# Gated recurrence and convolution gate on one core: decay constants without the logarithm table, and another written-out order

## The chip, the cores and the metric

The kernel runs on one core of a Trainium2 chip. The metric is device microseconds of one execution, lower is better. Three runs of the kernel before the change took 296.58, 295.05 and 296.55 us; their median, 296.55 us, is the time before.

The engines are called by the names of the profile: PE (TensorE; PEld is its weight load), DVE (VectorE), ACT (ScalarE), POOL (GpSimd) and SP (SyncE, which here only issues transfers). A q behind a name is that engine's queue.

## What is computed

Four sequences of 6336 tokens with 256 channels, all in float32. A recurrence with a data-dependent decay is followed by a gated linear unit:

```
a_base = sigmoid(a_param)
log_a  = 8 * sigmoid(r_gate) * log(clip(a_base, 1e-6, 1 - 1e-6))
a_t    = exp(log_a)
x_gated = sqrt(max(1 - a_t * a_t, 1e-6)) * sigmoid(i_gate) * x
h[t] = a_t[t] * h[t-1] + x_gated[t]            # y = h, zero at the start of a sequence
gate = sigmoid(sum over k < 5 of conv_w[k] * y[t - 4 + k])
out  = (gate * (y @ w_val)) @ w_out            # both 256 x 256
```

Sigmoids are computed as (1 + tanh(z/2))/2, so that the factor of the exponent is khf = 4 * log(clip(a_base)), and a_t = exp(khf * tanh(r/2) + khf).

## The kernel before

The 25,344 tokens are cut into 51 windows (two of 256 tokens at the start, one at the end, all others 512), and these into 28 chunks: chunks 0, 1, 2 and 26, 27 are one window each, and every other chunk c is the two windows 2c-3 and 2c-2. Square roots are taken in 12 batches of up to three chunks, because each needs ACT's square-root table and the way back needs the table of Exp and Tanh: two switches a batch. Batches 0 to 3 share one pair, so the loop makes 18 table loads (L518), and the setup makes two (L186, L234).

Tokens lie on the partitions when they are loaded, and channels on the partitions for the recurrence, so PE transposes three times. The work on a window or chunk is a chain of small operations, each a function op_xx of the code with a two-letter word:

- SP: lr, li, lx load r_gate, i_gate and x of a window (L278) into rings of four windows each; st stores a window (L502). s_wl.0 to s_wl.3 load the weights (L252 to L258).
- ACT: ta and tb, the tanh of the r and i gates of a chunk (L296, L299); ex, the Exp that reads the transposed tanh from PSUM (L359); rt, the square roots of a batch (L386); tg, the tanh of the convolution's result (L458); ca, a copy of a result from PSUM (L491); sa, a square (L375).
- POOL: pp, 1 + tanh of the i gate (L306); up, that times x (L318); sq, squares of a_t (L367); s_wcast, the weights to bfloat16.
- PE: tr, transposes of ta's result (L343); nt, of the square roots (L401); xt, of the gated x (L417); cv, the convolution as products with diagonals (L451); vl (L466) and ou (L481), the two matrix products; xp, x into PSUM.
- DVE: xg, the square root times the gated x (L408); sc, the recurrence as a scan of half the channels (L439); gv, gate times value (L471); cd, a copy of a result from PSUM (L489); uv, the gated x of a few early windows (L332).

The chain is lr, ta, tr, ex, sq, rt, nt, xg (with li, tb, pp, lx, up beside it), xt, sc, then cv, tg, vl, gv, ou, cd or ca, st. In a word such as ex.4.1@6,7 the first number is the chunk (of lr, li, lx, pp, up, cv, tg, vl, gv, ou, ca, cd and st: the window; of rt: the batch), the second the half of the channels, and the numbers behind the @ are PSUM banks.

The order is written out by hand: ORDER is a list of 961 words, and the loop behind it (L513) issues them one after the other. Each engine runs its own words in the order in which they stand, and waits with semaphores for what it needs; no scheduler moves anything. So the list sets five queues, the banks (which decide whose readers a matmul must wait for) and, by ca or cd, the engine of each copy. SP's queue holds loads and stores alike: a store that waits for its copy holds the loads that stand behind it, and a load waits until its slot in the ring is free, which for lr and li is when ta or tb of the window four before is done, and for lx when its product is.

The decay constants are made in s_kt: PE turns a_param onto the partitions, ACT takes an Exp, DVE three small operations, ACT a logarithm from the table set natural_log_exp_and_others (loaded at L186), then the set exp_and_others is loaded (L234) and DVE multiplies by 4.

Of the kernel before, what the change touches and what calls it, by code (L numbers as in the profile page):

```python
# [8 lines left out]
P = 128  # L9
CONV_K = 5  # L10
FP32 = mybir.dt.float32
BF16 = mybir.dt.bfloat16
ACT = mybir.ActivationFunctionType
ALU = mybir.AluOpType

CHUNKS = [[256], [256], [512], [512, 512], [512, 512], [512, 512], [512, 512], [512, 512], [512, 512], [512, 512], [512,
    512], [512, 512], [512, 512], [512, 512], [512, 512], [512, 512], [512, 512], [512, 512], [512, 512], [512,
    512], [512, 512], [512, 512], [512, 512], [512, 512], [512, 512], [512, 512], [512], [256]]
BATCHES = [[0], [1], [2], [3, 4], [5, 6, 7], [8, 9, 10], [11, 12, 13], [14, 15, 16], [17, 18, 19], [20, 21, 22], [23, 24,
    25], [26, 27]]  # L20
# [11 lines left out]
GROUPS = [[0], [1], [2], [3, 4], [5, 6], [7, 8], [9, 10], [11], [12], [13, 14], [15, 16], [17, 18], [19, 20], [21], [22],  # L32
    [23, 24], [25], [26], [27]]

ORDER = """
s_ident s_small s_kt s_diag lr.0 ta.0 lr.1 ta.1 li.0 tr.0.1@0 tb.0 pp.0 tr.0.0@1 ex.0.1 tr.1.0@2 tr.1.1@3 lr.2 ta.2
ex.1.0 tr.2.1@0 ex.1.1 ex.2.1 tr.2.0@2 lr.3 lr.4 lr.5 ex.0.0 ta.3 lr.6 ta.4 li.1 tr.3.1@0,1 lx.1 tb.1 sq.2.1 sq.1.1
sq.0.1 ex.2.0 li.2 tr.3.0@2,3 li.4 lx.0 li.3 tb.2 xp.1@4 sq.0.0 sq.1.0 sq.2.0 up.0 uv.1 lr.7 lr.8 ex.3.1 sq.4.1 ex.3.0
sq.3.0 lr.9 lr.10 lx.2 lx.4 s_wl.2 lx.3 li.5 li.6 s_wl.1 tb.3 s_wl.3 s_wl.0 ta.5 lx.5 ta.6 lr.14 rt.0 xp.2@2,3 nt.0@4
xg.0 xt.0@0,1 li.8 li.7 uv.2 rt.1 rt.2 nt.1@4 nt.2@5 xg.2 xg.1 pp.4 sq.3.1 sq.4.0 lx.6 rt.3 lr.11 tb.4 lr.12  # L40
tr.5.0@6,7 ex.5.0 xt.1@5,4 li.9 lr.13 sc.0.0 sc.0.1 pp.3 up.4 lx.8 nt.3@2,3 xt.2@0,1 sc.1.0 li.10 up.3 sc.1.1 xg.3
xt.3@2,3 tb.5 cv.1@4,5 sc.2.1 lx.7 sc.2.0 tg.1 cv.0@6,7 tg.0 tr.5.1@0,1 ex.5.1 s_wcast vl.1@4,5 sc.3.1 sc.3.0 xp.6@6,7
vl.0@0,1 nt.4@2,3 li.12 pp.5 ta.7 lr.16 sq.5.0 sq.6.0 up.5 li.11 ta.8 pp.8 uv.6 tb.6 gv.0 ou.0.0@0 lr.15 cv.2@6,7 tg.2
# [58 lines left out]
def kernel(  # L102
# [11 lines left out]
    nc = tc.nc  # L114
    B, S, D = x.shape
    H = D // P
# [63 lines left out]
    const = ctx.enter_context(tc.tile_pool(name="const", bufs=1))  # L180
# [4 lines left out]
    with tc.manual_schedule():  # L185
# [4 lines left out]
        khf = const.tile([P, H], FP32, name="khf")  # L190
# [359 lines left out]
```

## Time and profile before

| what | before |
|---|---|
| three runs, median | 296.55 us (295.05 to 296.58) |
| span of the profiled execution, first to last instruction | 294.6 us |
| the three runs above that span | 0.5 to 2.0 us |
| ACT busy | 277.3 us, 202 instructions |
| DVE, POOL, PE busy | 241.5, 241.8, 241.6 us |
| moved by DMA | 104.7 MB, mean 355 GB/s |
| mean granted PE clock | 0.990 |

The profile is one execution; a time of its own, besides the span, is not given with it. Engines run beside each other, so busy times are not added. A row of the timeline is: start in us, length in us, engine, line, operation, tile written and tile read with shapes, and in brackets the idle time of the engine just before and what ended it. A row with xN holds N instructions that followed each other. Rows on ACT overlap by about 0.1 us, so that two tanh rows of 1.91 us start 1.80 us apart. A row of the stretches gives the width in us, then busy us and instruction count of PE, PEld, DVE, ACT and POOL, the granted clock, the busy share of the DMA engines (it can pass 1 where packets overlap) and GB/s.

### The profile page before, as it was taken

Reading aid. Unit: us, or ns where it says so; the run is one execution under the profiler, and the core shown is the slowest. Engines: PE = TensorE matmul, PEld = TensorE weight load, DVE = VectorE, ACT = ScalarE, POOL = GpSimd, SP = SyncE. Lnnn points to the kernel's source line nnn. Section 1 sums busy time; section 2 is a strip of 40 time slices with the busy share of each in tenths; the row PEclk is TensorE's granted clock in tenths of the full one; section 3 lists DMA queues with packets and bytes.
Section 4 is the critical chain, followed back from the end, with each engine's and each line's share of the span. In section 5 each row is a group of like instructions: output and inputs, shape, how many; then the busy total and the mean of one; then the engine's idle time right before and its main releaser. Section 6 shows DMA issues by size and latency. Waiting matters only on the chain.

```text
span 294.6 us, 6238 instructions
## 1 busy us (share of the span) xinstructions
PE 241.6 (82%) x2497; PEld 165.2 (56%) x2497; DVE 241.5 (82%) x198; ACT 277.3 (94%) x202; POOL 241.8 (82%) x161
## 2 busy tenths in 40 slices
PE   2263879778697899988969889989889998899993
PEld 1241556436464767666636647566648674767652
DVE  2000697867999899997999998999999999999981
ACT  6799999999999999999999899999999999999754
POOL 1559979999999799999997989999997999666200
PEclk9999999999999999997999999999999999999998
DMA  7999999999999999999988999999999999965336
GB/s 242 336 414 388 383 408 401 403 412 376 414 398 405 401 383 388 392 356 417 385 257 312 364 411 414 415 350 406 374 389 384 392 331 369 346 249 209 153 142 249
DMA packets 29994, 104.74 MB, mean 355 GB/s; under 512 B 3335, under 2 KB 3854, under 8 KB 29966
## 3 DMA queue, kind: packets, MB, share of 16 engines
q1 hardware_dynamic: 29952, 104.35, 92.5%
q8 instruction: 19, 0.31, 0.4%
q14 instruction: 9, 0.07, 0.1%
q10 hardware_dynamic: 14, 0.01, 0.0%
HBM read 78.39 MB, written 25.95 MB: 354 GB/s over the span
## 4 chain that ended last, share of the span: by engine, by line
ACT 38%; DMA 23%; PE 20%; issue 12%; DVE 4%; SPq 1%; ACTq 0%; DVEq 0%
DMA rring<-in_r_gate_dram 10%; DMA iring<-in_i_gate_dram 9%; ACT aring L359 7%; ACT tgring L458 7%; ACT taring L296 7%; ACT ering L386 6%; ACT tbring L299 6%; PE banks L466 5%; PE banks L481 4%; PE banks L451 4%; ACT L518 4%; DMA xring<-in_x_dram 4%; PE banks L401 2%; PE banks L417 2%; DVE tgring L471 2%
## 5 line engine op out<-in xcount | busy, mean ns | idle before, releaser
L439 DVE TENSOR_TENSOR_SCAN yring<-aring,yring,banks 128x1024 bf16<-128x1024 f32 (+5 forms) x54 | 106.2, 1991 | 2.1 <-PE banks L417 1.9
L318 POOL TENSOR_TENSOR uring<-tbring,xring 128x1024 bf16<-128x1024 bf16 (+1 forms) x48 | 100.8, 2117 | 8.2 <-DMA xring<-in_x_dram 4.8
L367 POOL TENSOR_TENSOR ering<-aring 128x1024 f32<-128x1024 f32 (+2 forms) x54 | 91.5, 1714 | 11.7 <-ACT aring L359 11.6
L451 PE MATMUL banks<-yring,diag 64*64 64x512 bf16 (+7 forms) x1080 | 62.2, 362 | 3.0 <-DVE yring L439 1.1
L471 DVE SCALAR_TENSOR_TENSOR tgring<-tgring,banks 128x1024 bf16<-128x1024 bf16 (+1 forms) x51 | 59.0, 1179 | 5.7 <-ACT tgring L458 3.6
L306 POOL TENSOR_SCALAR tbring<-tbring 128x1024 bf16<-128x1024 bf16 (+1 forms) x48 | 48.9, 1030 | 13.1 <-ACT tbring L299 11.3
L481 PE MATMUL banks<-wo,tgring 128*128 128x256 bf16 x396 | 51.2, 274 | 8.3 <-DVE tgring L471 7.5
L359 ACT ACTIVATE aring<-banks,khf 128x2048 f32<-128x2048 bf16 (+3 forms) x38 | 54.5, 1472 | 1.6 <-PE banks L343 1.5
L466 PE MATMUL banks<-yring,wv 128*128 128x512 bf16 (+4 forms) x216 | 51.1, 366 | 4.7 <-ACT tgring L458 2.2
L458 ACT ACTIVATE tgring<-banks 128x1024 bf16<-128x1024 f32 (+1 forms) x51 | 49.7, 1008 | 3.4 <-PE banks L451 3.3
L481 PEld LDWEIGHTS <-tgring 128*128 128x128 bf16 x396 | 41.5, 114 | 18.7 <-DVE tgring L471 13.6
L296 ACT ACTIVATE taring<-rring 128x2048 bf16<-128x2048 f32 (+2 forms) x28 | 47.8, 1721 | 1.9 <-DMA rring<-in_r_gate_dram 1.9
L299 ACT ACTIVATE tbring<-iring 128x2048 bf16<-128x2048 f32 (+2 forms) x28 | 48.0, 1720 | 0.6 <-DMA iring<-in_i_gate_dram 0.5
L386 ACT ACTIVATE ering<-ering 128x4096 bf16<-128x4096 f32 (+5 forms) x15 | 44.7, 3016 | 0.1
L451 PEld LDWEIGHTS <-diag 64*64 64x64 bf16 x1080 | 29.0, 106 | 26.8 <-issue 10.7
L408 DVE TENSOR_TENSOR uring<-banks,uring 128x2048 bf16<-128x2048 bf16 (+2 forms) x28 | 30.3, 1095 | 15.9 <-PE banks L401 13.4
L489 DVE COPY oring<-banks 128x1024 f32<-128x1024 f32 (+1 forms) x33 | 38.3, 1183 | 5.5 <-PE banks L481 5.1
L343 PE MATMUL banks<-ident_b,taring 128*128 128x128 bf16 x396 | 30.1, 230 | 15.1 <-ACT taring L296 10.4
L343 PEld LDWEIGHTS <-taring 128*128 128x128 bf16 x396 | 26.1, 103 | 21.1 <-ACT taring L296 12.0
L466 PEld LDWEIGHTS <-wv 128*128 128x128 bf16 x216 | 19.7, 98 | 26.2 <-issue 13.1
L401 PE MATMUL banks<-ident,ering 128*128 128x128 f32 x198 | 30.0, 297 | 5.3 <-ACT ering L386 2.9
L401 PEld LDWEIGHTS banks<-ident,ering 128*128 128x128 f32 x198 | 26.9, 208 | 11.2 <-ACT ering L386 5.6
(37 smaller groups left out, 126.0 us busy)
## 6 DMA issues: line engine op xcount, KB each, us to landing
rring<-in_r_gate_dram SPq DMA_DIRECT2D x48, 512.0 KB, 7.6
iring<-in_i_gate_dram SPq DMA_DIRECT2D x48, 512.0 KB, 7.6
xring<-in_x_dram SPq DMA_DIRECT2D x48, 512.0 KB, 7.9
out_dram<-oring SPq DMA_DIRECT2D x48, 512.0 KB, 5.2
rring<-in_r_gate_dram SPq DMA_DIRECT2D x3, 256.0 KB, 3.0
iring<-in_i_gate_dram SPq DMA_DIRECT2D x3, 256.0 KB, 3.2
xring<-in_x_dram SPq DMA_DIRECT2D x3, 256.0 KB, 6.4
out_dram<-oring SPq DMA_DIRECT2D x3, 256.0 KB, 5.7
```

What stands on the lines that cost most here:

```text
L296: nc.scalar.activation(**tangent(c, taring, NTR, rring, NRI))
L299: nc.scalar.activation(**tangent(c, tbring, NTI, iring, NII))
L318: nc.gpsimd.tensor_tensor(out=u, in0=t1, in1=xt, op=ALU.mult)
L359: nc.scalar.activation(out=dst, in_=src, func=ACT.Exp, scale=khf[:, h:h + 1], bias=khf[:, h:h + 1])
L367: nc.gpsimd.tensor_tensor(out=e, in0=a, in1=a, op=ALU.mult)
L401: nc.tensor.transpose(out=bank[:, k:k + P], in_=ering[:, e + q:e + wins[w] // 2:nq], identity=ident[:])
L439: nc.vector.tensor_tensor_scan(out=yring[:, h, col:col + o1 - o0], data0=aring[:, h, a_at[c] + o0:a_at[c] + o1], data1=xT[:, o0:o1], initi ...
L451: nc.tensor.matmul(out=gp[oh * 64:oh * 64 + 64, h, a:b], lhsT=diag[half * 64:half * 64 + 64, h, k, :], rhs=yring[half * 64:half * 64 + 64, ...
L458: nc.scalar.activation(out=tgring[:, w % NTG, :, 0:wins[w]], in_=live.pop(("gp", w))[:, :, 0:wins[w]], func=ACT.Tanh, scale=0.5)
L466: nc.tensor.matmul(out=val[:, m, a:b], lhsT=wv[:, hk, m * P:(m + 1) * P], rhs=yring[:, hk, col:col + b - a], start=(hk == 0), stop=(hk == ...
L471: nc.vector.scalar_tensor_tensor(out=tgring[:, w % NTG, :, 0:wins[w]], in0=tgring[:, w % NTG, :, 0:wins[w]], scalar=1.0, in1=live.pop(("va ...
L481: nc.tensor.matmul(out=ops[:, j * D:(j + 1) * D], lhsT=gv[:, hk, j:wins[w]:J], rhs=wo[:, hk, :], start=(hk == 0), stop=(hk == H - 1))
```

## The change

Two things are changed, and nothing in tiles, rings, chunks, batches or groups (those lists are only wrapped differently).

First, s_kt makes khf without the logarithm: with z = exp(-|a|), log(sigmoid(a)) = min(a, 0) - log(1 + z), and log(1 + z) is the series 2 (f + f^3/3 + ... + f^15/15) with f = z/(2 + z). ACT keeps one Exp of 128 x 2, and DVE has 17 instructions of that size in place of 4. The setup loads one table set, exp_and_others.

Second, ORDER is another list of the same 961 words but for five: the copies of windows 8, 23, 33, 34 and 49 are cd in place of ca, so there are 13 ca and 38 cd where there were 18 and 33. Every queue and most bank numbers differ. Shown are the list's beginning and its end. Table switches by the loop stay 18.

```diff
...
+LOG_TERMS = [15, 13, 11, 9, 7, 5, 3]
...
 ORDER = """
-s_ident s_small s_kt s_diag lr.0 ta.0 lr.1 ta.1 li.0 tr.0.1@0 tb.0 pp.0 tr.0.0@1 ex.0.1 tr.1.0@2 tr.1.1@3 lr.2 ta.2
-ex.1.0 tr.2.1@0 ex.1.1 ex.2.1 tr.2.0@2 lr.3 lr.4 lr.5 ex.0.0 ta.3 lr.6 ta.4 li.1 tr.3.1@0,1 lx.1 tb.1 sq.2.1 sq.1.1
-sq.0.1 ex.2.0 li.2 tr.3.0@2,3 li.4 lx.0 li.3 tb.2 xp.1@4 sq.0.0 sq.1.0 sq.2.0 up.0 uv.1 lr.7 lr.8 ex.3.1 sq.4.1 ex.3.0
-sq.3.0 lr.9 lr.10 lx.2 lx.4 s_wl.2 lx.3 li.5 li.6 s_wl.1 tb.3 s_wl.3 s_wl.0 ta.5 lx.5 ta.6 lr.14 rt.0 xp.2@2,3 nt.0@4
...
-ou.39.0@4,5 ca.39.0 tr.27.0@0 tr.27.1@1 ex.27.1 ex.27.0 lx.50 lx.48 cv.42@2,3 up.47 tg.42 st.39 cv.41@4,5 tg.41
-sc.23.0 up.48 ou.40.0@0,1 ca.40.0 st.40 sa.27.1 vl.41@2,3 gv.41 vl.42@4,5 gv.42 tr.26.1@6 sq.27.0 tr.26.0@7 ex.26.0
-xt.24@0,1 sc.24.0 ex.26.1 sq.26.1 sc.24.1 tb.26 pp.49 sq.26.0 ou.41.0@2,3 ca.41.0 cv.43@4,5 cv.44@6,7 vl.43@2,3 tg.43
-ou.42.0@4,5 tg.44 rt.11 st.41 lx.49 nt.25@6,7 ca.42.0 gv.43 vl.44@0,1 xg.25 ou.43.0@2,3 xt.25@6,7 ca.43.0 gv.44
-cv.46@4,5 tb.27 tg.46 cv.45@2,3 tg.45 sc.25.1 sc.25.0 st.42 ou.44.0@0,1 ca.44.0 nt.26@7 st.43 st.44 up.49 xg.26
-vl.46@4,5 gv.46 vl.45@2,3 gv.45 cv.47@0,1 tg.47 ou.46.0@4,5 ca.46.0 xt.26@6,7 sc.26.0 ou.45.0@0,1 vl.47@2,3 ca.45.0
-st.45 nt.27@4 cv.48@5,6 tg.48 sc.26.1 cv.49@0,1 tg.49 gv.47 pp.50 up.50 xg.27 xt.27@5,4 sc.27.1 vl.49@2,3 ou.47.0@6,7
-ca.47.0 st.46 vl.48@0,1 gv.49 ou.49.0@2,3 ca.49.0 sc.27.0 st.47 cv.50@6,7 tg.50 gv.48 st.49 ou.48.0@0,1 ca.48.0 st.48
-vl.50@2,3 gv.50 ou.50.0@2 ca.50.0 st.50
+s_ident s_small s_kt s_diag lx.1 lr.1 lr.2 lr.0 ta.0 li.0 s_wl.1 lr.3 li.1 ta.1 lr.4 tr.1.0@0 tr.0.1@1 tb.0 tr.0.0@2
+lr.5 ta.2 ex.0.1 lr.6 tr.2.1@3 ex.1.0 ex.2.1 sq.0.1 sq.1.0 xp.1@4 tr.2.0@5 lx.0 lx.3 li.4 s_wl.3 li.3 li.2 lx.2
+tr.1.1@0 ta.3 ex.2.0 s_wl.0 sq.2.0 pp.0 sq.2.1 ta.4 up.0 ex.1.1 tr.3.1@6,7 ex.0.0 lr.8 s_wl.2 sq.1.1 sq.0.0 tb.1
+tr.3.0@0,1 ex.3.1 ex.3.0 uv.1 tb.3 xp.2@6,7 sq.3.1 sq.4.1 tb.2 li.5 lr.10 uv.2 sq.3.0 li.6 lr.9 li.7 lr.7 sq.4.0
+lx.4 li.8 lx.6 rt.2 lx.5 rt.0 rt.1 pp.3 up.3 s_wcast pp.4 nt.2@6 xg.2 rt.3 nt.1@7 nt.0@0 xg.0 xg.1 xt.0@0,1 sc.0.0
+sc.0.1 xt.1@6,7 sc.1.0 sc.1.1 xt.2@4,5 cv.0@0,1 vl.0@6,7 cv.1@2,3 sc.2.1 tg.0 vl.1@0,1 gv.0 lx.7 ta.5 up.4 sc.2.0
...
+sq.23.0 pp.43 sq.24.1 sq.25.0 tg.38 ex.25.1 xt.22@6,7 sc.21.1 sc.21.0 tg.37 ou.36.0@4,5 tb.24 sa.25.1 vl.38@0,1
+cd.36.0 cv.39@2,3 gv.38 st.36 lx.46 li.48 tg.39 sc.22.0 li.50 ou.38.0@0,1 vl.39@4,5 vl.37@2,3 pp.46 pp.44 rt.10
+up.44 up.43 cd.38.0 up.46 gv.37 ou.37.0@2,3 pp.45 cv.40@0,1 sc.22.1 st.38 lr.49 li.47 li.49 lr.50 cv.41@6,7 gv.39
+cd.37.0 nt.23@4,5 st.37 lx.48 vl.41@2,3 up.45 tg.41 xg.23 tg.40 vl.40@6,7 gv.41 nt.24@4,5 gv.40 xt.23@2,3
+ou.41.0@0,1 lx.50 lx.47 ta.26 tb.25 ta.27 pp.47 pp.48 up.47 xg.24 ou.39.0@6,7 ca.41.0 cv.42@4,5 sc.23.1 ca.39.0
+st.41 ou.40.0@0,1 st.39 tg.42 ca.40.0 vl.42@6,7 tr.27.0@3 ex.27.0 xt.24@4,5 tb.26 st.40 sc.23.0 tr.26.0@3 gv.42
+cv.44@0,1 pp.49 ex.26.0 lx.49 ou.42.0@6,7 tr.26.1@3 tg.44 sc.24.1 tr.27.1@2 ca.42.0 ex.26.1 sc.24.0 cv.43@0,1
+nt.25@6,7 sq.26.0 up.48 xg.25 ex.27.1 sq.27.0 up.49 vl.43@2,3 tg.43 sa.27.1 tb.27 cv.45@4,5 pp.50 sq.26.1 gv.43
+tg.45 st.42 vl.45@6,7 gv.45 vl.44@0,1 xt.25@4,5 gv.44 ou.45.0@6,7 rt.11 up.50 sc.25.1 ou.44.0@0,1 ca.45.0 ca.44.0
+st.45 ou.43.0@2,3 ca.43.0 nt.26@6 st.44 sc.25.0 vl.46@0,1 cv.46@2,3 st.43 nt.27@7 tg.46 xg.26 xg.27 cv.48@4,5
+xt.26@2,3 gv.46 tg.48 cv.47@6,7 tg.47 ou.46.0@4,5 sc.26.0 sc.26.1 vl.47@0,1 ca.46.0 gv.47 st.46 vl.48@6,7 xt.27@4,5
+cv.49@2,3 vl.49@0,1 gv.48 tg.49 sc.27.0 ou.48.0@6,7 gv.49 ou.47.0@2,3 sc.27.1 ca.48.0 ou.49.0@0,1 st.48 ca.47.0
+cv.50@4,5 cd.49.0 st.47 vl.50@2,3 tg.50 gv.50 ou.50.0@2 st.49 ca.50.0 st.50
 """
...
 
     with tc.manual_schedule():
-        nc.scalar.preload_act_table_set("natural_log_exp_and_others")
+        nc.scalar.preload_act_table_set("exp_and_others")
         ident = const.tile([P, P], FP32, name="ident")
         ap2 = const.tile([H, P], FP32, name="ap2")
         wrow = const.tile([CONV_K, D], FP32, name="wrow")
         khf = const.tile([P, H], FP32, name="khf")
         ksig = const.tile([P, H], FP32, name="ksig")
+        ktmp = const.tile([P, 4, H], FP32, name="ktmp")
         wcol = const.tile([P, H, CONV_K], FP32, name="wcol")
         diag = const.tile([P, H, CONV_K, 64], BF16, name="diag")
         wv = const.tile([P, H, D], BF16, name="wv")
@@ -225,14 +229,22 @@
         def s_kt():
             kps = banks[:, 0]
             nc.tensor.transpose(out=kps[:, 0:H], in_=ap2[0:H, :], identity=ident[0:H, 0:H])
-            nc.scalar.activation(out=ksig[:], in_=kps[:, 0:H], func=ACT.Exp, scale=-1.0)
-            nc.vector.tensor_scalar(out=ksig[:], in0=ksig[:], scalar1=1.0, scalar2=None, op0=ALU.add)
-            nc.vector.reciprocal(out=ksig[:], in_=ksig[:])
-            nc.vector.tensor_scalar(out=ksig[:], in0=ksig[:], scalar1=1e-6, scalar2=1.0 - 1e-6,
-                                    op0=ALU.max, op1=ALU.min)
-            nc.scalar.activation(out=ksig[:], in_=ksig[:], func=ACT.Ln)
-            nc.scalar.preload_act_table_set("exp_and_others")
-            nc.vector.tensor_scalar(out=khf[:], in0=ksig[:], scalar1=4.0, scalar2=None, op0=ALU.mult)
+            nc.vector.tensor_copy(out=ksig[:], in_=kps[:, 0:H])
+            z, f, f2, p = (ktmp[:, k] for k in range(4))
+            nc.vector.scalar_tensor_tensor(out=z, in0=ksig[:], scalar=-1.0, in1=ksig[:], op0=ALU.mult, op1=ALU.max)
+            nc.scalar.activation(out=z, in_=z, func=ACT.Exp, scale=-1.0)
+            nc.vector.tensor_scalar(out=ksig[:], in0=ksig[:], scalar1=0.0, scalar2=4.0, op0=ALU.min, op1=ALU.mult)
+            nc.vector.tensor_scalar(out=f, in0=z, scalar1=2.0, scalar2=None, op0=ALU.add)
+            nc.vector.reciprocal(out=f, in_=f)
+            nc.vector.tensor_tensor(out=f, in0=f, in1=z, op=ALU.mult)
+            nc.vector.tensor_tensor(out=f2, in0=f, in1=f, op=ALU.mult)
+            nc.vector.tensor_scalar(out=p, in0=f2, scalar1=1.0 / LOG_TERMS[0], scalar2=None, op0=ALU.mult)
+            for k in LOG_TERMS[1:]:
+                nc.vector.scalar_tensor_tensor(out=p, in0=p, scalar=1.0 / k, in1=f2, op0=ALU.add, op1=ALU.mult)
+            nc.vector.scalar_tensor_tensor(out=p, in0=p, scalar=1.0, in1=f, op0=ALU.add, op1=ALU.mult)
+            nc.vector.scalar_tensor_tensor(out=p, in0=p, scalar=-8.0, in1=ksig[:], op0=ALU.mult, op1=ALU.add)
+            nc.vector.tensor_scalar(out=khf[:], in0=p, scalar1=4.0 * math.log(1e-6),
+                                    scalar2=4.0 * math.log(1.0 - 1e-6), op0=ALU.max, op1=ALU.min)
 
         def s_diag():
             wps = banks[:, 1]
```

## Prediction

> **What bounds the kernel now.** I read the page's busy shares first, then ScalarE's (ACT's) timeline for every gap, then the stretches of 20 us for who is full when, then SP's waits, then the last 25 us of all engines.
>
> ```profile
> span 294.6 us, 6238 instructions
> PE 241.6 (82%) x2497; PEld 165.2 (56%) x2497; DVE 241.5 (82%) x198; ACT 277.3 (94%) x202; POOL 241.8 (82%) x161
> q1 hardware_dynamic: 29952, 104.35, 92.5%
> ```
>
> ACT leaves 17.3 us idle of 294.6. Where they lie is in its timeline:
>
> ```profile
> 4.19 1.28 ACT L234 ACT_TABLE_LOAD   x1
> 5.49 1.15 ACT L296 ACTIVATE taring<-rring 128x512 bf16<-128x512 f32 x2
> 7.84 1.06 ACT L296 ACTIVATE taring<-rring 128x1024 bf16<-128x1024 f32 x1 [0.23 <-DMA rring<-in_r_gate_dram]
> 11.89 1.91 ACT L296 ACTIVATE taring<-rring 128x2048 bf16<-128x2048 f32 x1 [0.96 <-DMA rring<-in_r_gate_dram]
> 14.46 1.91 ACT L296 ACTIVATE taring<-rring 128x2048 bf16<-128x2048 f32 x1 [0.66 <-DMA rring<-in_r_gate_dram]
> ...
> 268.18 1.49 ACT L386 ACTIVATE ering<-ering 128x1536 bf16<-128x1536 f32 x1
> ...
> 291.07 0.58 ACT L491 COPY oring<-banks 128x512 f32<-128x512 f32 x1 [0.88 <-PE banks L481]
> ```
>
> The reader is to see three stages. Up to 14.46 (ta.4) ACT idles 4.4 us, the last part of it on loads. From there to 277 it waits only 3.4 us in all (0.94, 0.77, 0.60, 0.55, 0.22 and slivers). From 277.9 the pipe drains: 6.3 us of waits and 2.95 us behind its last copy. So in the long middle ACT is the bound, but a second resource is as full:
>
> ```profile
> core 0: us, PE busy (x) PEld busy (x) DVE busy (x) ACT busy (x) POOL busy (x), PEclk, DMA share, GB/s
> 100.00:120.00 20.00, 18.88 (x239) 13.57 (x239) 19.26 (x16) 20.00 (x16) 17.95 (x11) 1.00 1.00 390
> 140.00:160.00 20.00, 17.21 (x178) 11.00 (x175) 19.47 (x14) 19.34 (x11) 18.44 (x12) 1.00 0.88 329
> 200.00:220.00 20.00, 17.07 (x194) 11.56 (x193) 20.00 (x14) 19.94 (x16) 20.00 (x13) 1.00 1.02 393
> 260.00:280.00 20.00, 20.00 (x211) 13.81 (x210) 19.22 (x15) 17.49 (x19) 9.68 (x8) 1.00 0.48 187
> ```
>
> The transfers stand at a share of 1.00 or more and 385 to 405 GB/s in every 20 us from 20 to 140, so whatever ACT gains has little feed to spare. Only 140 to 160 shows them starved, and there it is SP, whose one queue issues loads and stores in order:
>
> ```profile
> SPq L502 <- DVE oring L489: 62.8, 22, 6.9
> SPq L502 <- ACT oring L491: 43.3, 14, 6.2
> ```
>
> A store that waits for its copy holds every load behind it.
>
> **The change, part by part.** Costs on ACT are start-to-start spacings of the rows: tanh of 512, 1024, 2048 elements 0.53, 0.95, 1.80 us; Exp of 256, 512, 1024, 2048 elements 0.52, 0.70, 1.10, 1.95; gate tanh and output copy 0.91 (0.53 for 256 tokens); table switch 1.29; square roots as their rows.
>
> 1. *Decay constants.* ACT loses the Ln (0.20) and the second table load (1.28); before, ta.0 started at 5.49, 0.02 after that load. VectorE gets 17 tiny instructions for 4. At the 0.20 us from one to the next seen in L229 to L231, from the transpose's end at 3.14, with Exp at 3.6, khf is ready near 6.7 instead of 4.38, diag near 8 instead of 5.4. Their first users, ex.0.1 and cv.0, come near 11 and 31 by the working below, so I cost the chain at nothing; without that cover it would cost 2.3 us.
>
> 2. *The first loads.* This is what stands in the place of the table load. SP issued lr.0 first; now it issues lx.1, lr.1, lr.2, lr.0, and ACT still takes ta.0 first. The fourth load ends 1.31 MB, as lr.2 did before, and lr.2 landed at 7.84; so ta.0 starts at 7.8 (not before 6.0, when the stretches of 2 us show 1.3 MB moved). The rows say more at ta.4: its lr.6 ended 3.41 MB and landed at 14.46; now lx.1, li.1 and one weight load are ahead of it and it ends 4.06 MB. The 0.65 MB at the 331 to 401 GB/s of 12 to 16 us are 1.6 to 2.0 us: ta.4 at about 16.2. The work of ACT ahead of ta.4, counted from ta.0, is 7.1 us before and 6.8 after. So ACT's clock lies at 14.5 - 7.1 = 7.4 us before and 16.2 - 6.8 = 9.4 after: 2.0 us lost (bounds 0, if ta.4 finds its load as early as before, and 2.3, if lr.6 lands 0.9 MB behind the bytes moved, as lr.4 did at 11.89, so at 16.5).
>
> 3. *POOL and the first square roots.* rt.3 now comes without ta.5 and ta.6 ahead of it, so its squares must be ready 3.6 us of ACT work earlier. POOL: sq.2.0 after ex.2.0 at 16.0, then pp.0, sq.2.1, up.0, two small squares to 21.1 (0.62 to 1.16 each), sq.3.1 after ex.3.1 at 21.5, four squares of 1.9: 29.0. ACT reaches rt.3 at 29.8. Covered by 0.8 us; if not, the difference is lost one for one. tg.0 then follows at 34.7, with cv.0 long done.
>
> 4. *Copies.* ca goes from 18 to 13, cd from 33 to 38: copies 8, 23, 33, 34 and 49 go to VectorE. ACT: 5 x 0.90 = 4.5 us less. From ta.0 to the end its work is 272.6 us before and 268.1 after; up to rt.11 it is 256.6 and 255.3, since fewer operations are left behind rt.11 (12 against 16). VectorE: 5 x 1.21 = 6.1 us more, to about 250. It had 14 us idle between 40 and 180, but under 1 us in 200 to 260, where copies 33 and 34 fall; I cost them at nothing, because its first chunk now starts about 2 us earlier (xg.0 behind rt.0 near 29), and keep 2.4 us for the bad end.
>
> 5. *All queues and banks.* Table switches stay 18 behind the setup, bytes the same. New bank numbers alter which reader a matmul waits for; the trace can't price that. ACT's waits in the middle are 3.4 us now: I keep 3.4, with 0 and 8 (as much again and a stall, below) as ends.
>
> 6. *The drain.* With the same 4.2 us of waits and slivers between ta.4 and rt.11 as before (268.18 - 256.6 - 7.4), rt.11 starts at 255.3 + 9.4 + 4.2 = 268.9, that is 0.7 later than before. Then by hand, from the rows of the last 25 us: tg.45 ends at 267.6; VectorE does gv.45, gv.44 to 269.9, sc.25 twice to 274.4, xg.26 and xg.27 to 275.4; ACT does rt.11 to 270.3, ca.45, ca.44, ca.43 and the table load to 274.3, tg.46 to 275.3; gv.46 to 276.5, sc.26 twice to 278.9, gv.47, gv.48 to 281.7, sc.27.0, gv.49 (waits for cv.49 and tg.49, 283.0) and sc.27.1 to 284.9; cv.50, tg.50, gv.50, ou.50, ca.50 to 289.0; and the 2.95 us behind the last copy: 292.0. The drain from rt.11 is 23.1 us against 26.4. Its bad end is PE: it was full from 260 to 280, and if it comes there late the 3.3 us are not gained.
>
> **Sum.** 294.6 + 2.0 (start) - 1.3 (work up to rt.11) - 3.3 (drain) = 292.0 us of span. The runs shown lie 0.5 to 2.0 us above the profiled execution's 294.6, their median 1.95 above; so 294.0 us as a run.
>
> **The rivals.** *Transfers set the pace.* The tightest place is tb.22: 84.4 MB stand ahead of it on SP, ACT wants it at 210.5 + 9.4 = 219.9, which asks for 387 GB/s from 2 us on. Before, 53.9 MB had gone by 140 us: 391. But over 20 to 260 it was 382, stall included. At 382 the load comes near 223 and with landing some 4 us late: span 296, a run of 298. For it speaks that tb.18 did wait (0.55 us at 171.6) at a demand of 386; against it that the gaps of SP's queue look smaller in the new order. The Trainium skill has a harder rule: DMA: Bandwidth & Descriptors, section Where 436 GB/s comes from, puts the HBM side at about 358 GB/s per core, by which 104.7 MB alone would take some 293 us (an estimate from the page's figure) and no order could gain. The trace disagrees, with 405 GB/s over 40 to 60 and 421 over 18 to 20; it adds nothing to this rival's chance.
>
> *Slower: stores block loads.* In the new order a store stands right behind its copy: on average 1.1 us of ACT work lies between the two words, 4.3 before. SP then meets more copies not yet made. The one such stall of before, slices of 257 and 312 GB/s around 147 to 162, cost (143 + 88)/400 x 7.4 = 4.3 us of transfers. One more cancels the gain, two make a span of about 300.6, a run of 302.5. For it speaks the 106 us that SP already waits for copies; against it that a queue of 7.6 us to landing covers most.
>
> *Faster still.* Each ACT operation's producer stands farther ahead: the least lead of a square root over its squares is 2.2 us of ACT work instead of 0, of the slowest tenth of tb over their loads 4.6 instead of 0. If the 3.4 us of waits vanish: 288.6 span, 290.6.
>
> *The change doesn't do what it says:* khf late, and ex.0.1 held to 11 or more; by part 1 it needs 4 us more than the chain has. 2 in 100.
>
> **How the numbers follow.** A measurement of this kernel tells about 0.5% (1.5 us) from no change. Chances: the forecast, 0.43; faster still, 0.15; transfers, 0.22; blocked loads, 0.18; khf late, 0.02. Faster by over 0.5% (under 295.1): 0.15 + 0.36 = 0.51. Within 0.5%: 0.07 of the forecast and 0.16 of the transfers, 0.23. Slower: 0.06 + 0.18 + 0.02 = 0.26. The forecast's own range is 291 to 296; to hold 8 in 10 it reaches to 289.5 (waits gone and a start with no loss) and to 300 (transfers late, or between one stall and two).
>
> **What would show it.** ta.0 near 7.8 waiting for the rring transfer; ta.4 near 16; no Ln and 19 table loads; rt.11 starting near 269; ACT's busy time near 271; waits on ACT in the middle under 4 us; 23 us from rt.11 to the end. Waits of ACT on iring or rring after 140, or slices under 350 GB/s in the middle, show the transfers or the blocked loads; PE full past 282 shows the drain misjudged. I am wrong if ACT's middle waits exceed 6 us, or if ta.4 comes at 14.5.

## The result, and the profile after

The kernel after takes 300.98 us (median of four runs, 298.55 to 302.02), the kernel before 295.98 us beside it (295.05 to 296.58): a ratio of 1.0152 as it stands on record, with a 95% interval of 1.0112 to 1.0191 (the two medians alone give 1.0169). The change makes the kernel 1.5% slower; the prediction said 294.0 us and faster. The profiled execution of after has a span of 299.7 us and a time of 301.5, so it lies 1.8 us above its span, as the runs of before lay above theirs. All of the difference is in the span: 299.7 against 294.6.

The page's first lines of after (the line numbers of its operations are 12 higher than in before: L296 there is L308 here):

```profile
span 299.7 us, 6237 instructions
PE 244.4 (82%) x2471; PEld 167.8 (56%) x2497; DVE 250.0 (83%) x216; ACT 272.4 (91%) x195; POOL 241.8 (81%) x161
```

ACT does 4.9 us less work, as planned (277.3 to 272.4), and yet ends later: it idles 27.3 us where it idled 17.3. Its timeline says where (start, length, engine, line, operation, and in brackets the idle time ahead and what ended it):

```profile
8.38 1.15 ACT L308 ACTIVATE taring<-rring 128x512 bf16<-128x512 f32 x2 [4.62 <-DMA rring<-in_r_gate_dram]
...
15.81 1.91 ACT L308 ACTIVATE taring<-rring 128x2048 bf16<-128x2048 f32 x1
...
105.81 1.20 ACT L371 ACTIVATE aring<-banks,khf 128x1024 f32<-128x1024 bf16 x1 [0.81 <-PE banks L355]
...
158.22 1.91 ACT L308 ACTIVATE taring<-rring 128x2048 bf16<-128x2048 f32 x1 [0.71 <-DMA rring<-in_r_gate_dram]
...
180.25 1.91 ACT L308 ACTIVATE taring<-rring 128x2048 bf16<-128x2048 f32 x1 [2.51 <-DMA rring<-in_r_gate_dram]
...
210.27 1.92 ACT L311 ACTIVATE tbring<-iring 128x2048 bf16<-128x2048 f32 x1 [0.76 <-DMA iring<-in_i_gate_dram]
...
232.11 1.02 ACT L470 ACTIVATE tgring<-banks 128x1024 bf16<-128x1024 f32 x1 [0.91 <-PE banks L463]
...
244.29 1.91 ACT L311 ACTIVATE tbring<-iring 128x2048 bf16<-128x2048 f32 x1 [0.53 <-DMA iring<-in_i_gate_dram]
...
276.60 1.49 ACT L398 ACTIVATE ering<-ering 128x1536 bf16<-128x1536 f32 x1
...
296.07 0.58 ACT L503 COPY oring<-banks 128x512 f32<-128x512 f32 x1 [1.43 <-PE banks L493]
```

The reader is to see that the start (15.81 for ta.4) and the drain (276.60 to 299.7) are near the forecast, and that the loss lies between them. From 18 us to rt.11 the waits listed on ACT's rows add up to 9.4 us, where before had 3.1: 5.0 for loads (0.6 before), 3.3 for PE (1.8 before), 0.7 for a slot of the output ring (0.8 before) and 0.5 for its own. Of the 9.4 us, 8.1 lie behind 150 us. The stretches of 20 us (width; busy time and count of PE, PEld, DVE, ACT and POOL; clock; DMA share; GB/s):

```profile
core 0: us, PE busy (x) PEld busy (x) DVE busy (x) ACT busy (x) POOL busy (x), PEclk, DMA share, GB/s
...
140.00:160.00 20.00, 17.50 (x177) 11.00 (x177) 19.65 (x15) 19.23 (x12) 19.55 (x13) 1.00 1.00 381
160.00:180.00 20.00, 18.67 (x234) 15.04 (x232) 19.34 (x18) 17.74 (x13) 15.75 (x11) 1.00 0.98 375
...
220.00:240.00 20.00, 17.90 (x194) 13.26 (x200) 17.70 (x17) 18.53 (x14) 14.79 (x9) 0.91 0.89 334
...
260.00:280.00 20.00, 18.91 (x191) 13.26 (x191) 18.01 (x13) 18.29 (x22) 13.73 (x11) 1.00 0.49 189
```

No single stage carries it: ACT, which before was busy for 19.9 or more of most stretches, is at 17.7 to 19.2 in these. The stretch in which the transfers are starved moved from 140:160 (share 0.88 and 329 GB/s before, 1.00 and 381 now) to 220:240 (0.97 and 381 before, 0.89 and 334 now). Over 20 to 260 us both kernels move nearly the same, 382 GB/s before and 379 now. In SP's waits (us in total, times, longest) the stores hold the queue longer, 131 us against 106:

```profile
SPq L514 <- DVE oring L501: 90.9, 36, 7.0
SPq L514 <- ACT oring L503: 40.1, 13, 8.1
```

One number per stage makes the kernels below comparable: ACT's *lateness*, the start of a batch's first square root less the ACT work that its word has ahead of it from ta.0 (the same count as the 7.4 and 9.4 us of the prediction's second part). It is from one profiled execution each; rt.11's start, the drain behind it (from there to the end) and the span are beside it, in us. How far one execution can lie off: the rows of after and its variants have the same first loads, and yet stand between 7.7 and 9.8 at batches 0 to 3.

| kernel | batches 0-3 | 5 | 7 | 8 | 10 | 11 | rt.11 at | drain | span |
|---|---|---|---|---|---|---|---|---|---|
| before | 7.4 | 7.4 | 9.2 | 10.8 | 11.1 | 11.6 | 268.2 | 26.4 | 294.6 |
| after | 9.0 | 9.8 | 11.2 | 14.8 | 18.8 | 21.3 | 276.6 | 23.1 | 299.7 |
| new order, old constants | 9.3 | 10.8 | 12.2 | 16.4 | 20.9 | 22.6 | 277.9 | 23.1 | 301.0 |
| after, stores later | 7.7 | 9.1 | 13.1 | 17.6 | 19.1 | 20.9 | 276.2 | 23.5 | 299.7 |
| after, filled and stores later | 9.0 | 10.6 | 14.4 | 17.2 | 20.5 | 23.4 | 278.7 | 23.5 | 302.2 |
| after, half stores | 9.3 | 10.4 | 10.7 | 13.9 | 16.2 | 17.4 | 272.7 | 22.8 | 295.5 |
| after, three taps | 9.8 | 10.8 | 11.6 | 13.7 | 17.4 | 18.1 | 273.4 | 21.6 | 295.0 |
| after, three taps and half stores | 9.2 | 9.3 | 9.6 | 12.9 | 15.3 | 16.1 | 271.4 | 21.2 | 292.6 |
| after, three taps and stores later | 9.4 | 11.2 | 15.0 | 18.8 | 20.2 | 21.5 | 276.8 | 22.1 | 298.8 |
| before, half stores | 7.2 | 8.6 | 8.9 | 9.4 | 9.7 | 10.2 | 266.8 | 26.1 | 292.9 |
| before, five copies on VectorE | 7.0 | 8.2 | 10.5 | 15.5 | 21.2 | 21.7 | 274.6 | 30.2 | 304.8 |
| before, stores right behind their copies | 6.1 | 6.8 | 14.2 | 16.9 | 26.1 | 33.4 | 290.0 | 26.5 | 316.5 |

### The profile page after: what moved, and what is told of

Read it like the earlier page. It is cut to its first block, busy times and chain, and to the rows that moved or that the text cites. A ratio compares the mean times of both kernels' runs of the same rounds, so it can differ in the third digit from the quotient of the medians.

```text
span 299.7 us, 6237 instructions
## 1 busy us (share of the span) xinstructions
PE 244.4 (82%) x2471; PEld 167.8 (56%) x2497; DVE 250.0 (83%) x216; ACT 272.4 (91%) x195; POOL 241.8 (81%) x161
## 4 chain that ended last, share of the span: by engine, by line
ACT 27%; DMA 20%; PE 19%; DVE 15%; issue 9%; POOL 6%; SPq 2%; ACTq 0%; DVEq 0%; POOLq 0%
DMA iring<-in_i_gate_dram 11%; DMA rring<-in_r_gate_dram 8%; DVE yring L451 7%; ACT ering L398 7%; ACT taring L308 7%; PE banks L463 5%; PE banks L493 4%; ACT tgring L470 4%; DVE oring L501 4%; PE banks L413 3%; PE banks L478 3%; ACT L530 3%; ACT tbring L311 3%; POOL ering L379 2%; ACT aring L371 2%
## 5 line engine op out<-in xcount | busy, mean ns | idle before, releaser
L463 PE MATMUL banks<-yring,diag 64*64 64x512 bf16 (+7 forms) x1080 | 63.2, 365 | 3.5 <-DVE yring L451 2.3
L308 ACT ACTIVATE taring<-rring 128x2048 bf16<-128x2048 f32 (+2 forms) x28 | 47.4, 1713 | 9.3 <-DMA rring<-in_r_gate_dram 8.7
L478 PE MATMUL banks<-yring,wv 128*128 128x512 bf16 (+7 forms) x190 | 49.1, 363 | 7.6 <-ACT tgring L470 3.8
L501 DVE COPY oring<-banks 128x1024 f32<-128x1024 f32 (+1 forms) x38 | 44.6, 1187 | 5.2 <-PE banks L493 4.4
L413 PE MATMUL banks<-ident,ering 128*128 128x128 f32 x198 | 30.7, 303 | 12.0 <-ACT ering L398 8.4
L355 PE MATMUL banks<-ident_b,taring 128*128 128x128 bf16 x396 | 30.3, 230 | 10.7 <-ACT taring L308 9.6
L413 PEld LDWEIGHTS banks<-ident,ering 128*128 128x128 f32 x198 | 26.5, 208 | 18.7 <-ACT ering L398 8.6
L478 PEld LDWEIGHTS <-wv 128*128 128x128 bf16 x216 | 20.0, 99 | 27.1 <-issue 13.7
```

What stands on the lines that cost most here:

```text
L308: nc.scalar.activation(**tangent(c, taring, NTR, rring, NRI))
L413: nc.tensor.transpose(out=bank[:, k:k + P], in_=ering[:, e + q:e + wins[w] // 2:nq], identity=ident[:])
L463: nc.tensor.matmul(out=gp[oh * 64:oh * 64 + 64, h, a:b], lhsT=diag[half * 64:half * 64 + 64, h, k, :], rhs=yring[half * 64:half * 64 + 64, ...
L478: nc.tensor.matmul(out=val[:, m, a:b], lhsT=wv[:, hk, m * P:(m + 1) * P], rhs=yring[:, hk, col:col + b - a], start=(hk == 0), stop=(hk == ...
```

## The experiments

Every ratio is to the kernel before, run beside it on the same chip, with its 95% interval.

### Which part of the change carries the loss

The constants alone, put into the kernel before:

```diff
-        nc.scalar.preload_act_table_set("natural_log_exp_and_others")
+        nc.scalar.preload_act_table_set("exp_and_others")
...
-            nc.scalar.activation(out=ksig[:], in_=kps[:, 0:H], func=ACT.Exp, scale=-1.0)
...
+            nc.vector.tensor_copy(out=ksig[:], in_=kps[:, 0:H])
...
```

> The kernel before with only the decay constants made on VectorE and one table set; the order stays that of before. The table load that goes ended at 5.47 us, but before its ta.2, ta.3 and ta.4 each waited for a load (0.23, 0.96 and 0.66 us, the last landing at 14.46), so all theories expect ta.4 at 14.4 to 14.6 again and a time within 0.3% of before. If the constants themselves made the changed kernel slow (khf late), this run is slower by over 1%.

Measured: 1.002 [0.9989, 1.0052], 296.71 us. The time is as forecast; ta.4 came at 13.50, earlier than the 14.4 to 14.6 forecast. The order alone is the reverse edit, the kernel after with the old s_kt:

> The changed kernel with the decay constants as before (Ln, two table sets): the new order alone. If the order is the whole cause, it is as slow as the changed kernel, ratio 1.010 to 1.020. If the constants have a part in the loss, it is under 1.008.

Measured: 1.0171 [1.0114, 1.0227], 300.24 us. The constants do nothing to the time that these intervals could show, as the prediction costed them, and the order has the whole loss. The third part, the five copies, put back to ACT in the new order (five words `cd.8.0`, `cd.23.0`, `cd.33.0`, `cd.34.0`, `cd.49.0` become `ca`):

> The changed kernel with the copies of windows 8, 23, 33, 34 and 49 back on ScalarE, at the same places of the order. Theory 1 (stores stand close behind copies on a full VectorE, SP waits for them with the loads behind) expects VectorE's copies earlier and a gain of 1 to 4 us: ratio 1.002 to 1.012, and fewer than 90.9 us of SP waiting for VectorE's copies. Theory 2 (the transfers' own rate sets the pace, whatever the engines do) expects ScalarE's 4.5 us more of work to vanish in its waits for loads: 1.012 to 1.018, with the waits of ta and tb for DMA shorter than 10.3 us. Theory 3 (ScalarE's work sets the pace still) expects 4 us more: 1.03.

Measured: 1.0257 [1.0186, 1.0329], 303.25 us. The forecasts of theories 1 and 2 miss; nearest is the third's. In the new order the copies on VectorE look like a gain: without them it is about 1% slower still, though the two intervals just touch. Putting the same five copies on VectorE in the old order went the other way:

```diff
-tg.10 ou.8.0@0,1 ca.8.0 ex.12.0 st.9
+tg.10 ou.8.0@0,1 cd.8.0 ex.12.0 st.9
...
```

> The kernel before with copies 8, 23, 33, 34 and 49 on VectorE, at the same places of its order: the copies' part of the change alone. If ScalarE's 4.5 us come off the bound of the old order: ratio 0.986 to 0.993. If VectorE, full from 200 to 260, takes them back (6.1 us more): 0.997 to 1.010.

Measured: 1.0314 [1.0261, 1.0366], 306.24 us, beyond both forecasts, though ACT's busy time fell from 277.3 to 274.0 us. Three rows of this kernel's timelines show the largest single part. On VectorE:

```profile
168.74 1.23 DVE L489 COPY oring<-banks 128x1024 f32<-128x1024 f32 x1 [3.33 <-DMA out_dram<-oring]
```

On PE:

```profile
171.15 1.87 PE L481 MATMUL banks<-wo,tgring 128*128 128x256 bf16 x8 [3.35 <-DVE uring L408]
```

On ACT:

```profile
173.05 1.01 ACT L491 COPY oring<-banks 128x1024 f32<-128x1024 f32 x1 [4.12 <-PE banks L481]
```

The copy of window 23, one of the five, waits 3.33 us on VectorE for its slot of the output ring (four windows, free when the store of the window four before is out); the gated x behind it (169.88) comes late, PE stands still for 3.35 us, and ACT for 4.12. In before the same copy waited for the same slot on ACT, for 0.77 us (168.23). Of the rest of the 9 us, ACT waits another 4.4 for PE at 239.50 and 245.41, and the drain is 3.8 longer; what makes PE late there was not followed. So the same five words gain about 3 us in one order (near the edge of the noise) and cost about 9 in the other: no fixed price per copy holds.

### Strength of the queue: stores moved by a few words

To see how strong the rival "stores block loads" is, in the kernel before each store was put right behind the word of its copy, so that 46 of the 51 have no load between the two words (22 in before, 39 in after):

```diff
-ex.7.1 cd.0.0 xt.4@1,0 st.0 gv.1 ou.1.0@4
+ex.7.1 cd.0.0 st.0 xt.4@1,0 gv.1 ou.1.0@4
...
```

> The kernel before with each store moved ahead to stand directly behind its copy's word, as most do in the changed order; nothing else moves. Theory 1 expects the loss from the other side: SP waits longer for copies than the 106 us of before, loads issued later, ScalarE waiting for DMA in the middle (1.3 us before), ratio 1.005 to 1.015. If the place of the stores is harmless: 0.997 to 1.003.

Measured: 1.0819 [1.0725, 1.0912], 321.18 us, with nothing else changed; the forecast was 1.015 at most. ACT's waits in this kernel:

```profile
ACT tbring L299 <- DMA iring<-in_i_gate_dram: 17.1, 8, 6.4
ACT taring L296 <- DMA rring<-in_r_gate_dram: 6.0, 5, 2.4
```

So loads behind waiting stores can cost far more than the whole effect. In the kernel after the same thing is seen in SP's own rows ahead of the 2.51 us wait at 180.25:

```profile
167.96 1.18 SPq L290 DMA_DIRECT2D xring<-in_x_dram  x2
171.50 0.34 SPq L514 DMA_DIRECT2D out_dram<-oring  x1
172.19 1.07 SPq L290 DMA_DIRECT2D rring<-in_r_gate_dram  x2
```

SP issues nothing from 169.1 to 171.5, waiting for the copy that the store needs (on VectorE, it ends at 171.47); the loads of r_gate for that tanh leave only from 172.19 on. The other three load waits of over 0.5 us look the same. SP stands 2.6, 3.4 and 4.1 us ahead of the stores of windows 16, 29 and 35; each leaves within 0.03 us of the end of its copy, at 148.16, 202.73 and 237.81; and the loads for which ACT waits at 158.22, 210.27 and 244.29 leave behind it, at 150.98, at 203.12 and from 238.21 on. So all four waits, 4.5 of the 5.0 us, are for loads that stood behind a waiting store.

### Undoing the suspected waits in the new order

Each store of after was moved behind up to two of the loads that follow it, so that these loads leave sooner:

```diff
-ou.1.0@0 xg.3 st.0 lr.14 tr.5.1@4,5
+ou.1.0@0 xg.3 lr.14 tr.5.1@4,5
...
-cv.2@0,1 sc.3.0 lr.11 vl.2@2,3
+cv.2@0,1 sc.3.0 st.0 lr.11 vl.2@2,3
...
```

> The changed kernel with each store moved behind up to the two next loads on SP's queue (never past another store, nor past the copy that writes its buffer again); nothing else moves. Theory 1 expects SP to wait less for copies (131 us in all in the changed kernel) with loads held behind, ScalarE's waits for DMA between 100 and 265 us (5.7 us) to fall under 3, and 2 to 5 us gained: ratio 0.998 to 1.008. Theory 2 expects the same bytes at the same rate: 1.012 to 1.018. A store that comes too late would hold its copy's buffer: waits of copies on out_dram over 3 us, and no gain.

Measured: 1.0216 [1.0176, 1.0255], 302.2 us. What the edit aimed at came: SP waits 82 us for copies instead of 131, and ACT's waits for loads from 18 us on fell from 5.0 to 1.3. But the time did not fall, since PE's share of ACT's waits rose from 3.3 to 6.4. This is the last outcome of the forecast: two copies on VectorE wait for their slots, 2.51 us at 95.03 and 2.99 us here:

```profile
157.57 1.23 DVE L500 COPY oring<-banks 128x1024 f32<-128x1024 f32 x1 [2.99 <-DMA out_dram<-oring]
```

PE's row behind it:

```profile
158.85 1.83 PE L462 MATMUL banks<-yring,diag 64*64 64x512 bf16 x20 [2.47 <-DVE oring L500]
```

And ACT's:

```profile
160.72 1.02 ACT L469 ACTIVATE tgring<-banks 128x1024 bf16<-128x1024 f32 x1 [2.24 <-PE banks L462]
```

Read in this order: a store that leaves later frees its slot of the output ring later, so a copy on VectorE waits 2.99 us; PE's next product needs the banks that this copy reads, and waits 2.47; the gate's tanh on ACT waits 2.24. The copies of after wait only 0.4 us for slots on VectorE, and those of before not at all. The edit thus made a new wait of its own.

The other suspect was PE, which in after stands still while ACT takes square roots. One of its rows in after:

```profile
97.63 2.87 PE L413 MATMUL banks<-ident,ering 128*128 128x128 f32 x16 [2.43 <-ACT ering L398]
```

The clock behind it, in stretches of 2 us (columns as above):

```profile
98.00:100.00 2.00, 2.00 (x15) 2.00 (x14) 1.84 (x2) 1.99 (x3) 2.00 (x2) 0.70 0.97 389
100.00:102.00 2.00, 2.00 (x11) 1.67 (x9) 1.58 (x4) 2.00 (x3) 2.00 (x2) 0.50 1.03 420
```

The same transposes in before:

```profile
96.15 2.19 PE L401 MATMUL banks<-ident,ering 128*128 128x128 f32 x16 [0.88 <-ACT ering L386]
```

PE waits 2.43 us instead of 0.88, its granted clock falls to 0.50, and the 16 transposes take 2.87 us instead of 2.19. To keep the clock up, eight products of 128 x 512 whose result nobody reads were put ahead of the first nt of batches 4 to 10:

```diff
...
+                for _ in range(8):
+                    nc.tensor.matmul(out=bank[:, 0:512], lhsT=ident_b[:], rhs=wv[:].rearrange("p h d -> p (h d)"),
+                                     start=True, stop=True)
...
```

> The changed kernel with eight products of 128x512 (thrown away) on TensorE ahead of the first nt of each batch from 4 to 10, into the bank that this nt writes afterwards, so that TensorE doesn't stand still while ScalarE takes the square roots. In the changed kernel it stood still 2.61, 2.43 and 2.58 us before 66.6, 97.6 and 221.3, and the granted clock was 0.50 in the 3 to 4 us behind each. Theory 4 (lulls of TensorE behind the square roots lower its clock on the path) expects no clock under 0.9 at 68 and 98 us, ScalarE 1 to 3 us earlier at batch 10 (21.3 us behind its own work at batch 11 now), ratio 1.003 to 1.010. If the clock doesn't matter: 1.013 to 1.018. If the products delay nt: over 1.018.

> The same products and each store moved behind up to two loads as before (that run had ScalarE's waits for DMA down but clocks of 0.50 at 98 to 104 and 158 to 162 us). Theories 1 and 4 together (blocked loads and lowered clock are two parts of the loss) expect both gains: ratio 0.990 to 1.003, ScalarE's lag at batch 11 under 17 us. If something else is behind the loss: above 1.010.

> The kernel of the run ahead of this, with the first loads in the order of before (lr.0, lr.1, li.0, lr.2 and on; lx.1, li.1 and the first weight load behind lr.6, and xp.1 behind tr.3.0 on TensorE). The start's term, 1.65 us in the profiles (ta.4 at 14.46 before against 15.81 with 0.3 us less work ahead of it), should come off: 1 to 2 us less than the run ahead of this, ta.0 at 4 to 5 us and ta.4 at 14.4. If later stages swallow it: same time within 0.2%.

Measured: 1.0251 [1.0176, 1.0326] for the filled lulls, 1.0288 [1.0224, 1.0352] with the later stores as well, 1.0255 [1.0166, 1.0344] with the first loads in the old order besides. The clock drops behind the lulls at 68, 98 and 222 us went away with the filling (others came up at 72 and 188 instead), and nothing was gained: the products take PE's time (busy 254.8 us against 244.4), and ACT's waits for loads rose from 5.0 to 7.1 us and those for PE from 3.3 to 4.4. This is the third outcome of the first forecast: at 157.83 and 223.26 the eight products run, for 1.7 us, ahead of an nt whose square roots are done. So the edit does not price the clock by itself.

Two other things say something of the clock. Executions of the filled kernel took 304.17 us at a mean clock of 0.964 and 304.23 at 1.000, so the drops do not carry its time. And a drop seems to cost something where it falls: where the clock fell between 97 and 105 us with the stores in their places (after, old constants, copies back on ACT, half of gv, three taps), ACT waits 0.41 to 1.02 us for the transposes that ex.11.0 reads behind it; with half stores and in the filled kernel, where the clock did not fall there, it does not.

The second and third of these kernels also carry the slot waits of the later stores (4.0 and 4.2 us on VectorE). In the third the start is 1.9 us earlier than in the second (batches 0 to 3 late by 7.1 instead of 9.0, about as far apart as executions with the same first loads can be), and by batch 11 both are about 23.5 late: in these two executions, what was won at the start did not reach the end.

### Taking work off one resource, in both orders

Each edit was made to after and to before, and the gap between the two shows how much of the new order's loss hangs on that resource. Left out are half of the rows of each store, two of the five taps of the convolution, and gv on half of the tokens of a window. (Where a text below says half of each store's columns, it is the same edit: half of the rows.)

```diff
...
-                              oring[:, w % NOSB, 0:J, :])
+                              oring[:, w % NOSB, 0:J // 2, :])
```

> The changed kernel with each store sending only half of its window's rows: half of the output isn't written, and 13 MB of 104.7 don't move. Read together with the next run. If the transfers and SP's queue carry the loss of the new order, this kernel gains more than its twin does, and the gap of 4.5 us between the orders closes to under 1.5 us or turns. If the loss lies between the engines, the gap stays 3 us or more though ScalarE's waits for DMA go.

> The kernel before with the same halved stores (half of the output isn't written). If transfers bound it too, it gains several us; if ScalarE is the bound, as its 3.4 us of waits say, it gains under 3 us.

```diff
-                for k in range(CONV_K):
+                for k in range(CONV_K - 2):
...
```

> The changed kernel with three of the five taps of the convolution: two fifths of the convolution's products are left out, some 25 us of TensorE. If TensorE (its clock granted at 0.977, and the waits of tg for cv of 6.5 us) carries the loss, the gap to its twin closes to under 1.5 us. If not, the gap stays at 3 us or more.

> The kernel before with three of the five taps of the convolution (two fifths of its products left out). With TensorE no bound in the middle, only the drain gains, since TensorE was full from 260 to 280: 2 to 5 us under before.

```diff
-            nc.vector.scalar_tensor_tensor(out=tgring[:, w % NTG, :, 0:wins[w]],
+            nc.vector.scalar_tensor_tensor(out=tgring[:, w % NTG, :, 0:wins[w] // 2],
...
```

> The changed kernel with gv on half of each window's tokens (the product of gate and value is left out for the other half), some 27 us less of VectorE's 250. Theory 5 (in the new order VectorE, with TensorE behind it, sets the pace of the middle: it runs dry while ScalarE takes the square roots, 7.3 us of xg waiting for nt against 3.8, and is full in between) expects 6 us or more gained, ratio to before under 0.995, and a gap to the next run of under 2 us. Theory 1 alone (blocked loads) expects part of it, since copies come earlier. If VectorE isn't it: a gain under 2 us, or one no larger than its twin's.

> The kernel before with the same half of gv left out. ScalarE is its bound: theory 5 expects 1 to 4 us, from the drain above all, ratio 0.985 to 0.997.

> The changed kernel with half of gv left out and each store moved behind up to two loads. If blocked loads and VectorE's load are two separate limits, this is faster than the first run of these by 2 us or more; if VectorE's late copies are what blocks the stores (one chain), both are equal within 1 us.

| left out | after | before | gap |
|---|---|---|---|
| nothing | 1.0152 | 1 | 1.5% |
| half of each store | 0.9992 [0.9957, 1.0027] | 0.9942 [0.9916, 0.9969] | 0.5% |
| two of five taps | 1.0094 [1.0053, 1.0134] | 0.998 [0.9945, 1.0015] | 1.1% |
| half of gv | 1.0118 [1.0041, 1.0195] | 1.0036 [1.0004, 1.0067] | 0.8% |
| half of gv, stores later | 1.0229 [1.0167, 1.0291] | | |

The intervals of the gaps are some 0.4 to 0.8% to either side, so only half stores close the gap clear of noise, to 1.5 us, the edge of the forecast by which transfers and SP's queue carry the loss. Three taps leave a gap of 3.4 us, as forecast for the case that TensorE doesn't carry it. VectorE's amount of work is the bound in neither order: 24.3 us less of busy time (250.0 to 225.7) leaves after at 1.0118, inside the interval of the unedited kernel, and 24.7 us less leaves before no faster. With the later stores besides, it is slower still and neither of the two forecasts came: two copies wait 7.7 us for their slots. Bytes of stores matter most, and the new order is the more sensitive one: it gains 1.6%, the old one 0.6%. With half the bytes no copy waits for its slot, and the waits for PE fell from 3.3 to 1.7, but those for loads stay at 4.2. In that execution the clock did not fall near 98 and 222 us as it did in after, so the fall in the waits for PE can't be laid to the bytes alone. Nor is it the rate of the transfers alone: with half the bytes SP still waits 140 us for copies, and ACT still waits for loads at 158.04 and 179.39. Three taps cut PE's part of ACT's waits from 3.3 to 1.4 us and the loads' from 5.0 to 3.0, but 2.6 us of waits for POOL's squares come up in their place.

### Both at once

The last theory was that two limits take over from each other, late loads behind blocked stores, and PE's queue behind the square roots. Then an edit that relieves both must give more than the two single ones together.

> The kernel after with two edits at once: three of the convolution's five taps (two fifths of its products are left out), and each store moved behind up to two of the loads that follow it. Alone, the three taps gave a ratio to before of 1.009 with ScalarE 18.1 us late at batch 11, and the later stores 1.022 with 20.9 us; the kernel after has 1.015 and 21.3 us, and the kernel before with three taps 0.998 and 10.2 us. Theory 6: two limits take over from each other, loads that are issued late behind stores that wait for their copies, and TensorE's in-order queue, which stands behind ScalarE's square roots and then runs at a lowered clock. By it the two edits together give much more than their sum: a ratio of 0.998 or less, and ScalarE at most 14 us late at batch 11. The rival, that the lateness of the new order has further causes in the order of the words of every engine: 1.005 to 1.015, and 17 us or more late.

> The kernel after with three of the convolution's five taps and with half of each store's columns (two fifths of the products are left out, and half of the output is not written). Alone, the half stores gave a ratio of 0.999 with ScalarE 17.4 us late at batch 11, the three taps 1.009 with 18.1 us; the kernel before with half stores has 0.994 and 10.2 us. Theory 6 (two limits, the transfers with their queue and TensorE's in-order queue): 0.990 or less, and at most 13 us late at batch 11, since both limits are relieved. The rival, that the lateness has further causes in the order of the words: 0.995 to 1.000, and 15 us or more late.

Measured: three taps with later stores 1.0101 [1.0035, 1.0168], 21.5 us late at batch 11: the rival's numbers. Three taps with half stores 0.9893 [0.9833, 0.9953]: the theory's ratio, but 16.1 us late where it said 13 at most. The lateness goes against the theory in both. Half stores alone took 3.9 us of it, three taps alone 3.2, both together 5.2, less than their sum and not more. In the time both together gain 2.6%, and the two alone 1.6 and 0.6, which is a sum within the noise; the ratio also has the shorter drain in it (21.2 us, 23.1 in after). The theory falls in this form. The first of the two kernels fails for the reason seen above, a copy that waits 3.33 us for its slot at 97.19 and another 2.87 at 159.42. In the second the slot waits and nearly all waits for PE are gone (0.7 us left), and this is what is left on ACT:

```profile
156.99 1.91 ACT L308 ACTIVATE taring<-rring 128x2048 bf16<-128x2048 f32 x1 [1.05 <-DMA rring<-in_r_gate_dram]
...
178.42 1.91 ACT L308 ACTIVATE taring<-rring 128x2048 bf16<-128x2048 f32 x1 [1.91 <-DMA rring<-in_r_gate_dram]
...
240.83 1.91 ACT L311 ACTIVATE tbring<-iring 128x2048 bf16<-128x2048 f32 x1 [1.05 <-DMA iring<-in_i_gate_dram]
```

These are three of the operations for which after waits, too (ta.17, ta.21 and tb.24, at 158.22, 180.25 and 244.29), 4.0 us in all where after has 3.8. Taking work off did not make their loads come in time; moving the stores behind loads took most of these waits away (1.3 us is left, at ta.21), and that ran into the output ring.

## Why the prediction was wrong

**The step that failed is part 5,** "I keep 3.4, with 0 and 8 (as much again and a stall, below) as ends", and with it the 4.2 us of waits and slivers that part 6 put between ta.4 and rt.11. The runs put 12.3 us there (276.60 - 15.81 - 248.5 of work): 10.3 us in which ACT is idle, against 3.6 before, and 2.0 against 0.6 in which rows take longer than their spacing back to back. By the prediction's own sum: 294.6 + 1.65 (start) - 1.3 (work) + 8.1 (waits) - 3.3 (drain) = 299.7. The one term that was kept has the size of the whole miss, and even its bad end was too short: the waits listed on ACT's rows alone are 9.4 us, beyond the 8, and beyond the 6 that the prediction named as its sign of being wrong. Part 5 left the new banks unpriced, since the trace can't price them, and kept the old sum; the new places of the stores came in only as a rival.

**The start was right in size.** ta.0 at 8.38 behind its load (7.8 forecast), ta.4 at 15.81 (16.2), 1.65 us lost for 2.0. That it fits to 0.4 us is in part luck: in this execution ta.4 did not wait for its load (the last wait of the start is ta.3's, 0.71 us), with half stores it did (1.08), and with the same first loads it came between 14.49 and 16.56. The constants cost nothing, shown by the run with them alone; there is no Ln and there are 19 table loads. tg.0 starts at 34.01 (34.7), so POOL's cover of the first square roots held.

**The copies were right in their count and wrong in their price.** ACT's busy time is 272.4 (271) and VectorE's 250.0 (about 250). But "I cost them at nothing" can't be said of the edit by itself: it gains about 3 us in the new order, near the edge of the noise, and costs about 9 us in the old one.

**The drain was right to the tenth,** 23.1 us from rt.11 to the end. PE was not full there (18.91 of 20 us from 260 to 280).

**The rivals.** "Slower: stores block loads" had the sign, and its 302.5 us for two stalls is nearest to the 300.98 measured. Its evidence, 1.1 us of ACT work between a copy's word and its store's instead of 4.3, should have weighed more than the queue of 7.6 us set against it. But it had only one half: the loads are 5.0 of the 9.4 us, PE is 3.3. "Faster still" argued that each producer stands farther ahead in ACT's work, so that waits vanish; they grew threefold. A lead counted on ACT's clock says nothing of how late SP, VectorE or PE reach the producer's word. "Transfers set the pace" is partly borne out, by the 1.6% that half stores give, but not as a rate alone: with half of the bytes ACT waits for late loads still, and tb.22, its tightest place, did not wait at all in after.

**What the runs show of the cause, and what stays open.** Shown: the loss is the order's; it builds up behind batch 7 above all (after is 2.0 us later than before at batch 7, 9.7 at batch 11); ACT waits there for loads that SP issues behind waiting stores, and for PE; and a store is bounded on both sides, since too early it holds loads and too late it holds, through the output ring, the copy four windows on and then VectorE, PE and ACT. Not shown: how much of the 8.1 us each of the two has on its own, since each edit that removed one wait made or uncovered another; how much of PE's part is its lowered clock; and so which words of the order would have to move. An output ring of more than four windows with the later stores would separate them; it wasn't tried. No variant was faster than the kernel before while doing all of its work.

## What to carry to other kernels

In a queue that carries loads and stores in order, ask of every store both questions: which load stands behind it while its copy isn't made, and which later copy waits for its slot if it leaves later. A new order of all queues can't be priced by keeping the old sum of waits, nor by leads counted on the busiest engine; it needs a replay of every queue with its rings and banks, and until there is one the range has to reach well past "as much again". The price of a moved operation belongs to the order in which it stands: measure it there.

## What was not expected of the hardware

TensorE's granted clock falls towards 0.50 behind standstills shorter than 3 us, and not each time. Behind the wait of 2.61 us at 66.56 in after the clock of the next 3.4 us is 0.73, behind the same wait of 2.61 us at 66.65 with half stores it is 1.00; 2.00 us at 76.38 (before, copies on VectorE) gave 0.68, 2.01 us at 75.58 in before gave 1.00. The Trainium skill, TensorE: Matmul & The Clock Gate, section Why this matters for your kernels, asks for no gaps above about 3 us, and its section What's actually happening says that the activity window is 3.4 us long and runs freely. The uneven outcome agrees with a free-running window; the limit of 3 us doesn't hold here, since 1.8 to 2.6 us were enough at times. One execution's drop need not be a property of the kernel: before has one at 135 to 139 us, behind a standstill of 1.77 us, and its lateness there grows by 1.7 us, but with the constants alone, in the same order and without the drop, by 0.2. Those near 100 us are hardly chance: of the ten kernels profiled in the new order without the filling, eight have one there.

That 24 us less work on VectorE, 83% busy in after, gave no time that the runs could show, and that moving stores by a few words costs 8%, were the two sizes farthest from what a reading of the busy shares suggests.
